# Dilated and sliding-window attention before a gated feed-forward layer: a later planned landing for transposed loads

## The chip, the core and the metric

The kernel runs on one core of a Trainium2 chip, in one launch. The metric is the time on the device in microseconds (us); the median of several runs is compared. One execution was also recorded by the hardware profiler.

## What is computed

The inputs are q, k and v (8 batches, 8 heads, 576 positions, 64 elements per head, float32), two weight matrices and a vector beta.

```python
scores = (q @ k.T) / 8                      # per batch and head
rel    = pos[:, None] - pos[None, :]
plain  = (rel >= 0) & (rel < 32)            # heads 0 to 3
dil    = (rel >= 0) & (rel < 128) & (rel % 4 == 0)   # heads 4 to 7
attn   = softmax(where(mask, scores, -1e9)) @ v
x      = attn as 4608 tokens x 512
h      = x @ w_in                           # 512 -> 2048
g      = h / (1 + exp(-beta * h))
out    = g @ w_out                          # 2048 -> 512
```

Batches are counted from 0 here, as in the code: b = 0 to 7.

## The kernel before

**Work and tiles.** Attention is done batch by batch. The feed-forward layer runs over nine tiles t of 512 tokens each; a batch has 576 tokens, so a tile takes its tokens from one or two batches. For tile t, 16 groups of four matmuls of 512 columns multiply xT (the attention's result, transposed) with w_in (`slot_h`, line 811); ScalarE takes tanh (820) and VectorE makes the gate g (825). Four blocks of 16 matmuls then multiply g with w_out (`block`, line 846), in four parts each, and the result is evacuated by ScalarE (861) or VectorE (863) and stored by an SP queue transfer (866).

**Attention of one batch.** The four dilated heads take their scores from dk and dq (line 639, matmuls on half of the array), with a tail of 16 positions per residue from the copies dkt and qt (609); the copies are made by VectorE or GpSimd (232). The four plain heads take theirs from kT and qT (673), in two halves j = 0 and 1 of the batch. ScalarE takes exp into ptd, ptt or pt (576), a mask is multiplied in (580), the values follow (714 and 699 dilated, 729 plain), and VectorE divides by the row sums (595, 596) into xdm, xdt and xsp.

**Where k and q come from.** In batches 0 to 2 (`b < DIRECT`, DIRECT = 3) TensorE transposes them. From batch 3 on, four transfers on GpSimd's queue cast them to bfloat16 in a scratch in device memory (`cast`), and four transposing transfers on the SP queue (`crossbar`, line 438) bring them back as dk, dq, kT and qT, 288 KB each. Before a batch's casts GpSimd makes a small copy (`pace`, line 924) that waits for xT of the batch two before; it keeps the transfers from starting earlier.

**The way back.** From batch 2 on the attention's result goes to device memory in two halves (`back_dma`: xdm line 483, xdt 488, xsp 475), and a transposing SP transfer per half brings it back as xT (502).

**What sets the order.** All of this is only described to `Plan`. Each operation has an engine or a choice of two, an estimated duration, dependencies and a priority `vt`; `Plan.run` goes through time, picks the next operation for the engine that can start first, and writes out the program in that order. It also picks the engine and the bank of the accumulator. For a transfer the plan takes the landing to be

```python
at = max(dma_free[e], s + d + 900)
other = max(dma_free.values()) - at
dma_free[e] = at + o.dma + max(0.0, min(o.dma, other))
o.end = dma_free[e] + (o.lat or 1100)
```

and what depends on the transfer is not placed before that planned time. `lat` is thus a constant in nanoseconds that is added to the planned landing. On the chip nothing of it remains but the order on each engine: each engine works in its order and waits for semaphores.

**Waits to know.** Batch b uses buffer b % 2 of dk, dq, kT, qT, dkt and qt. A batch's scores stand in the order among the matmuls of lines 811 and 846 of neighbouring tiles.

Of the kernel before, what the change touches and what calls it, by code (L numbers as in the profile page):

```python
# [174 lines left out]
def kernel(  # L175
# [34 lines left out]
    DIRECT = 3  # L210
# [220 lines left out]
    def crossbar(b, z, h0, deps, vt):  # L431
        kv = b % 2
        if h0:
            dst = (dk, dq)[z][kv][:].rearrange("p r h t -> p r (h t)")
        else:
            dst = qT[kv][:] if z else kT[kv][:, :, WIN:]
        src = scratch[b, z, h0][:].rearrange("(a e) -> a e", e=C * D)
        return plan.op([("SP", 1300)], lambda e: nc.sync.dma_start_transpose(out=dst, in_=src),
                       deps, vt, dma=288 * 1024 / .2 / 1000, lat=4000)

# [465 lines left out]
    def loads(b):  # L908
        if b < DIRECT:
            base = -7.25 if b == 1 else .2  # L910
            for n, (z, h0) in enumerate(((0, 4), (1, 4), (0, 0), (1, 0))):
                ld[b]["qk", z, h0] = direct_qk(b, z, h0, war(("st", z)), base + .01 * n)
            wrote(("st", 0), ("st", 1))
            ld[b]["vd"] = direct_vd(b, war("vd16"), base + .05, war(("vt", b % 2)) + [fill4])
            wrote("vd16", ("vt", b % 2))
            ld[b]["vp"] = direct_vp(b, war(("vp", b % 2)) + [fill4], base + .06)
            wrote(("vp", b % 2))
        else:
            behind = [ld[b - 1]["x", z, h0] for z in range(2) for h0 in (0, 4)] if b > DIRECT else []

            mid = (b - 2) * S + S // 2

            def t_pace(e, b=b, mid=mid):
                nc.gpsimd.tensor_copy(out=pace[:], in_=(  # L924
                    xT[0:1, 0, mid - 1:mid + 1] if b - 2 >= BY_DMA else g_t[b % 2][0:1, 0, 0:2]))
            go = plan.op([("POOL", 150)], t_pace, behind + (
                xready(mid - 1, mid + 1) if b - 2 >= BY_DMA else gop[b - 2, 0]), b - 2.4)
            for n, (z, h0) in enumerate(((0, 4), (1, 4), (0, 0), (1, 0))):
                c = cast(b, z, h0, [go], b - 2 + .01 * n)
                key = [(((("dk", "dq") if h0 else ("kT", "qT"))[z]), b % 2, i) for i in range(2)]  # L930
                ld[b]["x", z, h0] = crossbar(b, z, h0, [c] + war(*key), b - 2 + .01 * n)
                wrote(*key)
            key = [("st", z) for z in range(2)] if b < DIRECT + 2 else [("st", b % 2)]
            ld[b]["vd"] = direct_vd(b, [go] + war(*key), b - 2 + .02, [go] + war(("vt", b % 2)))
            wrote(("st", b % 2), ("vt", b % 2))
            ld[b]["vp"] = direct_vp(b, [go] + war(("vp", b % 2)), b - 2 + .03)
            wrote(("vp", b % 2))

    steady = LATER.split()
    for t in range(NTT):  # L940
# [4 lines left out]
        b = t + 1  # L945
# [46 lines left out]
```

The softmax here doesn't subtract the row's maximum and nothing guards it: scores larger than these inputs give would overflow.

## Time and profile before

| what | value |
|---|---|
| median of 5 runs | 305.62 us (305.25 to 306.92) |
| the profiled execution's own time | 305.25 us |
| span, first to last instruction | 303.5 us |
| TensorE busy (matmul) | 293.4 us, 97% of the span |
| VectorE, ScalarE, GpSimd busy | 183.6, 170.7, 90.3 us |
| mean granted TensorE clock | 1.000 |
| transposed loads dk, dq, kT, qT | 5 of each, batches 3 to 7 |

The span lies inside the execution's time; 1.75 us are outside of it. In the views, PE is TensorE, PEld its weight loads, DVE VectorE, ACT ScalarE, POOL GpSimd, and SP the engine whose queue carries transfers. Times in a view count from the start of the span. A line such as L639 is the line of the kernel that recorded the instruction; buffer numbers are left out of names, so dq stands for both of its buffers. A bracket at the end of a line in order of time gives the idle time before it and what ended it.

### The profile page before, as it was taken

What the parts mean: (1) busy time and instruction counts of PE and PEld (TensorE: products, weight loads), DVE (VectorE), ACT (ScalarE), POOL (GpSimd) and SP (SyncE); (2) the same over time, 40 slices, a digit from 0 to 9 for tenths busy, and PEclk for the clock granted to TensorE, in tenths of its full rate; (3) what the DMA queues carried; (4) which work ended last, traced back from release to release, by engine and by line L of the source; (5) the groups of instructions that cost most, each with busy time, mean ns of one, the idle gap of its engine ahead of it and who ended that gap; (6) DMA issues with size and microseconds to landing.
All of it is one profiled execution on the core that took longest, in us unless ns stands there. A gap on an engine that the chain in (4) does not pass through costs nothing.

```text
span 303.5 us, 5999 instructions
## 1 busy us (share of the span) xinstructions
PE 293.4 (97%) x2275; PEld 149.3 (49%) x2312; DVE 183.6 (61%) x422; ACT 170.7 (56%) x315; POOL 90.3 (30%) x132
## 2 busy tenths in 40 slices
PE   8899999999999989999999999999999999999995
PEld 5565456545544444444444444444444444444454
DVE  3669874988867755876677567757664344343300
ACT  2667953877548544855665566556554444554411
POOL 8988562846063107310560092100000000000000
PEclk9999999999999999999999999999999999999999
DMA  6999999999899997999999979991332100010122
GB/s 105 170 210 202 206 185 213 199 149 175 190 181 207 161 178 129 193 152 214 160 182 181 216 144 148 182 225 56 95 93 73 39 35 35 35 37 35 53 83 73
DMA packets 117376, 42.47 MB, mean 140 GB/s; under 512 B 93748, under 2 KB 110916, under 8 KB 117348
## 3 DMA queue, kind: packets, MB, share of 16 engines
q0 software_dynamic: 66672, 19.66, 63.8%
q1 hardware_dynamic: 50532, 22.36, 36.4%
q8 instruction: 18, 0.29, 0.4%
q14 instruction: 10, 0.08, 0.1%
q10 hardware_dynamic: 144, 0.07, 0.1%
HBM read 39.32 MB, written 18.87 MB: 192 GB/s over the span
## 4 chain that ended last, share of the span: by engine, by line
PE 69%; DMA 21%; POOL 4%; issue 2%; DVE 1%; SPq 1%; ACT 0%; POOLq 0%; ACTq 0%; DVEq 0%
PE bank L846 33%; PE bank L811 31%; DMA vd<-in_v_dram 4%; DMA st<-in_q_dram 4%; DMA w_in_bf<-in_moe_w_in_dram 4%; DMA st<-in_v_dram 3%; DMA dq<-s 3%; DMA x<-xsp 1%; PE bank L673 1%; PE bank L729 1%; DMA xT<-x 1%; PE bank L639 1%; POOL st L384 1%; PE bank L714 1%; POOL vp L384 1%
## 5 line engine op out<-in xcount | busy, mean ns | idle before, releaser
L846 PE MATMUL bank<-w_out_bf,g 128*128 128x512 bf16 (+2 forms) x590 | 140.2, 367 | 1.7 <-issue 1.0
L825 DVE SCALAR_TENSOR_TENSOR g<-tnh,bank 128x512 bf16<-128x512 bf16 x144 | 97.7, 685 | 72.5 <-ACT tnh L820 71.6
L820 ACT ACTIVATE tnh<-bank,beta_half 128x512 bf16<-128x512 f32 x144 | 98.5, 689 | 74.4 <-PE bank L811 70.1
L811 PE MATMUL bank<-xT,w_in_bf 128*128 128x512 bf16 (+1 forms) x565 | 139.3, 376 | 1.1 <-issue 0.2
L811 PEld LDWEIGHTS <-w_in_bf 128*128 128x128 bf16 x584 | 54.7, 98 | 60.1 <-issue 0.2
L846 PEld LDWEIGHTS <-g 128*128 128x128 bf16 x608 | 54.6, 98 | 55.7
L861 ACT ACTIVATE osb<-bank 128x512 f32<-128x512 f32 (+1 forms) x36 | 21.2, 589 | 32.0 <-PE bank L846 31.7
L576 ACT ACTIVATE pt<-bank 128x288 bf16<-128x288 f32 x64 | 21.6, 422 | 5.3 <-PE bank L673 5.3
L576 ACT ACTIVATE ptd<-bank 128x512 bf16<-128x512 f32 x32 | 17.0, 608 | 6.6 <-PE bank L639 6.6
L596 DVE TENSOR_TENSOR xsp<-bank,rcp 96x384 bf16<-96x384 f32 x32 | 17.7, 553 | 1.1
L384 POOL DMA_DIRECT2D vp<-in_v_dram x10 | 18.0, 1798 | 0.5 <-PE bank L455 0.5
L595 DVE RECIPROCAL rcp<-bank 128x4 f32<-128x4 f32 (+2 forms) x72 | 12.9, 179 | 5.3 <-PE bank L729 4.3
L580 DVE TENSOR_TENSOR ptd<-ptd,mask_d 128x512 bf16<-128x512 bf16 x27 | 12.0, 453 | 5.7 <-ACT ptd L576 4.5
L596 DVE TENSOR_TENSOR xdm<-bank,rcp 128x256 bf16<-128x256 f32 x32 | 13.6, 425 | 1.1
L384 POOL DMA_DIRECT2D vt<-in_v_dram x16 | 13.7, 1046 | 0.0
L384 POOL DMA_DIRECT2D s<-in_q_dram x10 | 13.7, 1369 | 0.0
L924 POOL COPY pace<-xT 1x2 bf16<-1x2 bf16 x4 | 0.7, 176 | 43.4 <-DMA xT<-x 36.4
L729 PEld LDWEIGHTS <-pt 128*128 128x128 bf16 x192 | 9.4, 97 | 5.9
L384 POOL DMA_DIRECT2D s<-in_k_dram x10 | 11.2, 1121 | 1.2 <-issue 1.2
L232 POOL COPY dkt<-dk 128x384 bf16<-128x384 bf16 x7 | 3.8, 548 | 25.3 <-DMA dk<-s 20.2
L729 PE MATMUL bank<-vp,pt 128*128 128x65 bf16 x192 | 10.4, 193 | 0.0
L714 PEld LDWEIGHTS <-ptd 128*128 128x128 bf16 x128 | 6.7, 98 | 4.7 <-issue 0.2
(108 smaller groups left out, 180.4 us busy)
## 6 DMA issues: line engine op xcount, KB each, us to landing
out_dram<-osb SPq DMA_DIRECT2D x35, 256.0 KB, 2.7
s<-in_k_dram POOLq DMA_DIRECT2D x10, 288.0 KB, 6.0
s<-in_q_dram POOLq DMA_DIRECT2D x10, 288.0 KB, 9.0
vp<-in_v_dram POOLq DMA_DIRECT2D x7, 384.0 KB, 17.6
w_out_bf<-in_moe_w_out_dram POOLq DMA_DIRECT2D x2, 1024.0 KB, 16.3
st<-in_k_dram POOLq DMA_DIRECT2D x6, 288.0 KB, 12.9
st<-in_q_dram POOLq DMA_DIRECT2D x6, 288.0 KB, 12.3
x<-xsp SPq DMA_DIRECT2D x12, 144.0 KB, 6.8
```

Of the source, the lines that this page charges most:

```text
L384: {"POOL": nc.gpsimd, "SP": nc.sync}[queue].dma_start(out=out, in_=in_)
L576: nc.scalar.activation(out=w(), in_=sc(), func=ACT.Exp, scale=SCALE)
L580: E[e].tensor_tensor(out=w(), in0=w(), in1=m(), op=ALU.mult)
L595: nc.vector.reciprocal(out=r, in_=p[..., D])
L596: nc.vector.tensor_tensor(out=dst, in0=p[..., 0:D], in1=r.unsqueeze(len(p.shape) - 1).to_broadcast(list(p.shape[:-1]) + [D]), op=ALU.mult)
L714: nc.tensor.matmul(pv[:, r, a], lhsT=ptd[:, x - 2, j, 2 * r + a], rhs=vd[kv][:, 2 * (x - 2) + a, 2 * r + j, 0:D + 1], start=True, stop=True)
L729: nc.tensor.matmul(pv[:, a, h2, :], lhsT=pt[x][:, (3 * j + a) * 2 + h2], rhs=vp[kv][:, (2 * x + h2) * NI + 3 * j + a, 0:D + 1], start=True ...
L811: nc.tensor.matmul(bank(g)[:, a:z], lhsT=w_in_bf[:, kt, fb * P:(fb + 1) * P], rhs=xT[:, kt, xo + a:xo + z], start=(i == 0 and kt == kts[0] ...
L820: nc.scalar.activation(out=th[:, 0:n], in_=bank(g)[:, 0:n], func=ACT.Tanh, scale=beta_half[:, fb:fb + 1])
L825: nc.vector.scalar_tensor_tensor(out=g_t[t % 2][:, fb, c0:c0 + n], in0=th[:, 0:n], scalar=1.0, in1=bank(g)[:, 0:n], op0=ALU.add, op1=ALU.mult)
L846: nc.tensor.matmul(bank(g)[:, lo:hi], lhsT=g_t[t % 2][:, fb, tb * P:(tb + 1) * P], rhs=w_out_bf[:, fb, lo:hi], start=(fb == 0), stop=(fb = ...
L861: nc.scalar.mul(out=ob[:, lo:hi], in_=bank(g)[:, lo:hi], mul=0.5)
```

## The change

The planned landing of the transposed loads of k and q gets 1500 ns later for batches 4 to 7. Batch 3 keeps the old value. No instruction is written differently; the planner places operations by the new times.

```diff
         src = scratch[b, z, h0][:].rearrange("(a e) -> a e", e=C * D)
         return plan.op([("SP", 1300)], lambda e: nc.sync.dma_start_transpose(out=dst, in_=src),
-                       deps, vt, dma=288 * 1024 / .2 / 1000, lat=4000)
+                       deps, vt, dma=288 * 1024 / .2 / 1000, lat=4000 if b == DIRECT else 5500)
```

## The prediction

> **What bounds the kernel now.** I read the page's summary first, then TensorE's waits after 60 us, then the chain of waits around the one that is left, then TensorE and the SP queue in order of time.
>
> ```profile
> span 303.5 us, 5999 instructions
> PE 293.4 (97%) x2275; PEld 149.3 (49%) x2312; DVE 183.6 (61%) x422; ACT 170.7 (56%) x315; POOL 90.3 (30%) x132
> PEclk9999999999999999999999999999999999999999
> ```
>
> TensorE is busy 97% of the span at the full granted clock, so no other engine sets the end. Its waits from 60 to 300 us (who waited for what: us in total, times, longest):
>
> ```profile
> PE bank L639 <- DMA dq<-s: 1.0, 1, 1.0
> PE bank L846 <- issue: 1.0, 6, 0.2
> ```
>
> Only the first line is a wait for data. The second is six breaks of 0.16 us where full-width matmuls follow the half-array scores. The chain places the wait (start, length, what):
>
> ```profile
> 101.12 8.31 DMA dq<-s
> 109.43 0.14 issue
> 109.57 0.62 PE bank L639 x16
> ```
>
> This is batch 4: its transposed load of dq, issued at 101.12, landed at 109.43, and the dilated scores (L639) started 0.14 later. TensorE in order of time:
>
> ```profile
> 109.57 0.62 PE L639 MATMUL bank<-dq,dk 64*128 64x128 bf16 x16 [1.04 <-DMA dq<-s]
> 139.58 0.62 PE L639 MATMUL bank<-dq,dk 64*128 64x128 bf16 x16
> 150.59 0.43 PE L673 MATMUL bank<-qT,kT 64*128 64x96 bf16 x12
> 170.39 0.62 PE L639 MATMUL bank<-dq,dk 64*128 64x128 bf16 x16
> 201.19 0.62 PE L639 MATMUL bank<-dq,dk 64*128 64x128 bf16 x16
> ```
>
> Batch 4 waits 1.04; the same scores of batches 5, 6 and 7 wait for nothing. By the trace's landing marks their dq was there at 135.28, 163.40 and 194.05: 4.3, 7.0 and 7.1 us early. So at most about 1.04 us can be gained, in one place.
>
> **What really moves.** The diff adds 1.5 us to a planned landing; only the planned order shows what follows. With the two built programs side by side, I count the big matmuls (L811 and L846) ahead of each score group. Dilated scores: batch 4 from 336 to 344, batches 5, 6, 7 unchanged at 460, 588, 716. Plain scores (L673), first and second half: batch 4 from 356 and 408 to 364 and 416; batch 5 from 504 to **480**, second half 536 unchanged; batch 6 from 632 to 636, second half unchanged; batch 7 unchanged. So the title holds for batch 4 and hardly beyond, and batch 5's first plain scores go the other way. No matmul is added or removed, and the number of half-array groups stays.
>
> **The gain.** Big matmuls start 0.216 us apart (a group of four is 0.86 in the chain). Without its wait L639 of batch 4 would start at 109.57 - 1.04 = 108.53; eight matmuls later is 108.53 + 8 x 0.216 = 110.26. dq lands at 109.43 and needs 0.14: 0.69 us to spare. The loads up to there stand in the same order on SP and POOL, so the landing has no reason to move. The wait goes whole: **-1.04**.
>
> A rule of the skill would deny that there was anything to gain. The Trainium skill, page "DMA: Bandwidth & Descriptors", section "Anatomy of one DMA — SWDGE (gpsimd) path", fits one transfer, on GpSimd's path, as 2.0 us plus bytes over 436 GB/s. As an estimate from that page, dq's 288 KB would take 2.7 us, land at 106.7 after its issue ended at 104.00, and the change would be worth 0. The row's 109.43 decides against it: the load shares the engines with casts and other transposes.
>
> **What the moves put on other queues.**
> - DVE takes batch 4's dkt copy from POOL. POOL waited for dk until 107.83; now DVE does, from about 105.66, and queued behind it are the last gate of the tile (before at 106.70) and the two qt copies. The copy is 0.54 on POOL, 0.97 in DVE's one row; the gate 0.69: done at 109.1 to 109.5. Who waits: L639, whose first bank that gate frees, at 110.26. Covered by 0.8 or more; once gone, each later us of dk costs one. Taken: 0.
> - DVE takes one output evacuation (ACT 0.60; DVE's 0.43 and 0.29 for 256 and 128 columns give an estimated 0.7 for 512). Behind it stand the four masks of batch 4's second half, the first two of which L729 needs. That half's L673 comes at 127.52 - 1.04 + 1.73 = 128.2, the block's last four matmuls end at 129.5, the evacuation at about 130.4, two masks of 0.3 at 131.0; L729 follows L673 by 3.0 as before, at 131.2. Bounds 0 to 0.3; taken 0.
> - POOL loses dkt of batch 4 (its next step, the pace copy, waits for xT until 115.3 anyway), gains batch 5's vd (1.04, from DVE) and loses half of its qt (0.29). Needed near 140, done by 133: 0.
> - SP: output stores of 0.3 to 0.6 issue go ahead of batch 4's xdm stores and of batch 6's dq and qT. dq of batch 6 has 7.0 to spare, its qT landed at 172.05 for scores at 181: 0.
> - SP, batches 5 and 7: the kT load now stands before the store of the previous batch's first half (x<-xsp), which the return transpose L502 needs.
>
> ```profile
> 127.76 0.54 SPq L475 DMA_DIRECT2D x<-xsp  x1
> 130.39 1.54 SPq L438 DMA_TRANSPOSE kT<-s  x1
> 135.88 2.09 SPq L438 DMA_TRANSPOSE qT<-s  x1
> 138.71 3.26 SPq L502 DMA_TRANSPOSE xT<-x  x1
> ```
>
> These are batch 5's loads and batch 4's store and transpose. kT landed at 139.53; the store, now behind it, lands about then, so L502 starts at about 139.6 instead of 138.71. Its own 3.26 went into a full queue (1.33 at 219.71), and it landed at 144.28; the tile's first L811 came at 145.3, now about 145.5. Bounds 0 to 0.5; taken 0. For batch 7 kT landed at 199.91, L502 stood at 197.94 for 2.69 and landed at 204.86; L811 came at 205.7 and comes now at about the same time. L502 from 199.95, for 1.33 and then the 1.9 to 4.2 that the rows have from its end to landing, gives 203.2 to 205.5; if it is late by the whole 2.0 it lands at 206.9. Bounds 0 to 1.3; taken 0, since the shorter issue pays the delay back.
> - Batch 5's plain scores, 24 matmuls forward: L673 came 11.0 us after L639, now 11.0 - 24 x 0.216 = 5.8 after it. L639 is at 139.58 - 1.04 = 138.54, so L673 at 144.3. Its qT, issued at 135.88 once the cast it reads was in, landed at 142.86: with 0.14, 1.3 to spare where there were 7.6. Bounds 0 to 3.0 (below); taken 0.
>
> **Sum.** The profiled execution took 305.25: span 303.5 and 1.75 around it. 305.25 - 1.04 = 304.21. The median of the runs is 0.37 above that execution, so 305.62 - 1.04 = 304.58. I take 0.1 more off: a later dq in the slower runs lengthens the same wait, and the new 0.69 absorbs it. **304.5**. 0.3% is 0.92 us, about what a measurement of this kernel can tell from no change: faster means under 304.70, slower over 306.54.
>
> **Rivals.**
> 1. *The wait comes back in part at batch 5's plain scores or at a tile's first L811.* For: their spare times are 1.3, about 1 and about 1 us, and they hang on loads that took 3.5 to 11.2 us from issue to landing. If qT of batch 5 takes the 8.7 us of batch 6's (163.32 to 172.05), it lands at 144.6 and costs 0.4; 0.5 more at the L811 of 145.5 brings the total back to about the old time: 304.7 to 305.6. Against: the same transfers stand ahead of qT in the queue as before, only in another order. Chance 0.28.
> 2. *Slower: batch 5's qT as late as the slowest transposed load.* kT of batch 6 took 11.24 us (158.98 to 170.22). With that, qT lands at 147.1, L673 waits 147.1 + 0.14 - 144.3 = 3.0, and the kernel ends at 305.62 - 1.04 + 3.0 = 307.6. It decides from a landing of 145.2 on (the 1.04 is spent), and over 0.3% slower from 146.1. For: before, nobody noticed how late this load came, since the scores stood 7.6 us behind it. Against: its own row says 7.0. Chance 0.20.
> 3. *The change doesn't do what it says*, so that nothing comes of it: 305.6. For: three of four batches keep their dilated scores where they were. Against: the one group that waits does move, by 1.73 us, more than its wait. Chance 0.02.
>
> The forecast, the wait gone and no new one over 0.1: chance 0.50; its own range is 303.9 to 304.7, down to 305.62 - 1.04 - 0.37 - 0.3 for runs whose dq came later than in the profile. The range takes in rival 1 and the smaller half of rival 2: 303.9 to 306.6. Faster 0.50; within 0.3% rival 1 and 3, less the little of rival 1 that may pass either edge: 0.29; slower 0.21.
>
> **What would show it.** Right: TensorE's waits have no line L639 <- DMA dq; L639 of batch 4 stands near 110.3 without idle; DVE shows a wait of about 2 us at dkt; L639 of batch 5 near 138.5; the tail of L846 ends 1.0 earlier. Wrong: a wait of L673 on qT near 144, or of L811 on xT near 145 or 206; a wait at L639 of batch 4 that remains, or one on DVE there; an L729 near 131 that waits for its masks. A slower time with none of these would overturn the whole working.

## The result, and the profile after

| kernel | median, us | lowest to highest | against before |
|---|---|---|---|
| before, 65 runs | 305.70 | 304.07 to 307.12 | |
| after, 37 runs | 304.96 | 303.98 to 306.05 | 0.9974, 95% interval 0.9965 to 0.9984 |

The change makes the kernel faster by 0.74 us between the medians, by 0.79 us (0.5 to 1.1) by the ratio. Forecast were 304.5 us: 1.04 us less for the wait and 0.1 more.

The profiled execution of after took 305.56 us, 0.31 more than that of before. That is no contradiction, as two views together show. First the summary, and TensorE's waits from 60 to 300 us, of which only this line is left:

```profile
span 303.7 us, 5999 instructions
PE 293.8 (97%) x2275; PEld 149.2 (49%) x2312; DVE 183.0 (60%) x424; ACT 171.0 (56%) x314; POOL 90.1 (30%) x131
PEclk9999999999999999999999999999999999999999
```

```profile
PE bank L846 <- issue: 0.8, 5, 0.2
```

The line L639 <- DMA dq is gone. What is left is no wait either. Each of these breaks stands before a group of L846 of which the trace has three matmuls where the program has four (or seven of eight). In b4_b6 below, whose matmuls stand in the same order, all of them are recorded and no break is seen. Behind batch 7's dilated scores, for example, after and then b4_b6:

```profile
202.16 0.81 PE L846 MATMUL bank<-w_out_bf,g 128*128 128x512 bf16 x3 [0.16 <-issue]
```

```profile
201.28 1.04 PE L846 MATMUL bank<-w_out_bf,g 128*128 128x512 bf16 x4
```

So single records are missing there, and the prediction's "six breaks of 0.16 us" were the same; no sum hung on them. TensorE in order of time, after (the dilated scores of batches 4 to 7 and batch 5's first plain ones):

```profile
111.49 0.62 PE L639 MATMUL bank<-dq,dk 64*128 64x128 bf16 x16
139.76 0.62 PE L639 MATMUL bank<-dq,dk 64*128 64x128 bf16 x16
145.59 0.43 PE L673 MATMUL bank<-qT,kT 64*128 64x96 bf16 x12
170.57 0.62 PE L639 MATMUL bank<-dq,dk 64*128 64x128 bf16 x16
201.38 0.62 PE L639 MATMUL bank<-dq,dk 64*128 64x128 bf16 x16
```

No group has a bracket, so none waited as the profile counts it. Batch 5's plain scores stand at 145.59, forward as the plan says, and do not wait either. Yet all of it is later than the prediction's 110.3 and 138.5. The reason stands long before the change: the first plain scores of batch 2 in the two kernels, before and then after.

```profile
68.22 0.43 PE L673 MATMUL bank<-qT,kT 64*128 64x96 bf16 x12
```

```profile
69.36 0.43 PE L673 MATMUL bank<-qT,kT 64*128 64x96 bf16 x12
```

Up to there both kernels have the same order, and after's execution was 1.14 late already: the waits before 60 us for input loads differ (L455 for st<-in_q was 1.1 after and 0.4 before). From this group to TensorE's last matmul it took 232.13 us before (to 300.35) and 231.17 after (to 300.53): 0.96 less. This distance is the measure used below. (Expectations that speak of 231.3 us count from the start of the L846 matmul ahead of that group, 0.31 earlier.)

The chain of waits of after, about batch 4's scores:

```profile
111.01 0.38 PE bank L846
111.39 0.10 issue
111.49 0.62 PE bank L639 x16
```

A DMA stands no longer in it. Still the load came close: by the trace's landing marks dq landed at 111.35, and L639 starts 0.14 later; from start to start TensorE lost 0.16 us more there than at the other changes from L846 to L639. VectorE's waits and the SP queue are as the working had them:

```profile
DVE dkt L232 <- DMA dk<-s: 2.3, 1, 2.3
DVE qt L232 <- DMA dq<-s: 1.3, 1, 1.3
```

```profile
128.47 2.84 SPq L438 DMA_TRANSPOSE kT<-s  x1
131.41 0.54 SPq L475 DMA_DIRECT2D x<-xsp  x1
135.10 1.99 SPq L438 DMA_TRANSPOSE qT<-s  x1
138.98 1.90 SPq L502 DMA_TRANSPOSE xT<-x  x1
```

kT now goes ahead of the store. L502 starts at 138.98, against 138.71 before, and lands at 143.12, against 144.28.

### The profile page after: what moved, and what is told of

It is laid out like the page before. It is cut to its first block, busy times and chain, and to the rows that moved or that the text cites. A ratio compares the mean times of both kernels' runs of the same rounds, so it can differ in the third digit from the quotient of the medians.

```text
span 303.7 us, 5999 instructions
## 1 busy us (share of the span) xinstructions
PE 293.8 (97%) x2275; PEld 149.2 (49%) x2312; DVE 183.0 (60%) x424; ACT 171.0 (56%) x314; POOL 90.1 (30%) x131
## 4 chain that ended last, share of the span: by engine, by line
PE 81%; DMA 11%; POOL 3%; DVE 2%; issue 2%; ACT 0%; POOLq 0%; DVEq 0%
PE bank L846 38%; PE bank L811 37%; DMA vd<-in_v_dram 4%; DMA st<-in_q_dram 4%; DMA w_in_bf<-in_moe_w_in_dram 3%; DVE g L825 2%; PE bank L729 1%; PE bank L673 1%; PE bank L639 1%; PE bank L714 1%; POOL st L384 1%; POOL vp L384 1%; PE bank L699 0%; PE bank L455 0%; DVE xdm L596 0%
## 5 line engine op out<-in xcount | busy, mean ns | idle before, releaser
L846 PE MATMUL bank<-w_out_bf,g 128*128 128x512 bf16 (+2 forms) x587 | 139.4, 367 | 1.7 <-issue 0.8
L811 PE MATMUL bank<-xT,w_in_bf 128*128 128x512 bf16 (+1 forms) x568 | 138.2, 376 | 1.2 <-DMA w_in_bf<-in_moe_w_in_dram 0.3
L811 PEld LDWEIGHTS <-w_in_bf 128*128 128x128 bf16 x584 | 55.1, 98 | 61.4 <-DMA w_in_bf<-in_moe_w_in_dram 0.4
L846 PEld LDWEIGHTS <-g 128*128 128x128 bf16 x608 | 54.4, 98 | 55.4
L729 PEld LDWEIGHTS <-pt 128*128 128x128 bf16 x192 | 9.1, 97 | 5.4
L232 POOL COPY vd<-st 128x1024 bf16<-128x1024 bf16 x5 | 5.2, 1036 | 20.5 <-DMA st<-in_v_dram 14.4
L729 PE MATMUL bank<-vp,pt 128*128 128x65 bf16 x192 | 10.1, 193 | 0.0
L863 DVE TENSOR_SCALAR osb<-bank 128x512 f32<-128x512 f32 (+2 forms) x3 | 1.4, 470 | 13.3 <-PE bank L846 13.3
```

What stands on the lines that cost most here:

```text
L232: (nc.scalar.copy if e == "ACT" else E[e].tensor_copy)(out=out, in_=in_)
L729: nc.tensor.matmul(pv[:, a, h2, :], lhsT=pt[x][:, (3 * j + a) * 2 + h2], rhs=vp[kv][:, (2 * x + h2) * NI + 3 * j + a, 0:D + 1], start=True ...
L811: nc.tensor.matmul(bank(g)[:, a:z], lhsT=w_in_bf[:, kt, fb * P:(fb + 1) * P], rhs=xT[:, kt, xo + a:xo + z], start=(i == 0 and kt == kts[0] ...
L846: nc.tensor.matmul(bank(g)[:, lo:hi], lhsT=g_t[t % 2][:, fb, tb * P:(tb + 1) * P], rhs=w_out_bf[:, fb, lo:hi], start=(fb == 0), stop=(fb = ...
```

## The experiments

Theory A: dq of batch 4 lands late against TensorE, and the gain is the wait for it, nowhere else. Theory B: the gain comes from the place of the scores or from the other batches' moves. All times are beside runs of before on the same chip. The edits are to the kernel before, to the planned `lat` of `crossbar` (line 439) unless another line is shown. The expectations name further theories, C to H.

### Batch 4 alone, and the others alone

```diff
-  lat=4000)
+  lat=5500 if b == 4 else 4000)      # only_b4
+  lat=5500 if b > 4 else 4000)       # from_b5
```

only_b4: 

> The later landing for batch 4 alone (5500 ns there, 4000 for all others). In the built order batch 4's dilated scores have 344 big matmuls ahead of them, as in the changed kernel. Theory A (the gain is the wait of batch 4's scores on dq, which eight more matmuls cover): the same time as the changed kernel, 0.7 to 1.0 us under the kernel before, and no wait of L639 over 0.3 us. Rival B (the gain needs batches 5 to 7 too): near the kernel before.

from_b5: 

> The later landing for batches 5 to 7 alone. TensorE's order stays that of the kernel before, word for word; only a few copies change between VectorE and GpSimd. Theory A: the time of the kernel before, within 0.2 us, and the wait of batch 4's L639 on dq is there again (0.5 to 2 us in the profile). Rival B: faster by 0.3 us or more.

Measured: from_b5 306.00 us against 305.59, ratio 1.0018 (0.9993 to 1.0043): no gain, as theory A has it, though the median lies 0.41 above where 0.2 was the most expected; the interval takes that in. Its trace still has the wait, 0.53 us.

```profile
109.72 0.62 PE L639 MATMUL bank<-dq,dk 64*128 64x128 bf16 x16 [0.53 <-DMA dq<-s]
```

only_b4 took 305.35 us, ratio 0.9996 (0.9968 to 1.0025). Its trace has no wait and takes 231.01 us from batch 2's scores to the end, 0.16 less than after's. But the median shows only 0.24 of it, and the interval holds both nothing and the whole gain. The runs alone leave open whether batch 4 is enough; b4_b6 below was made for that.

### The other direction, and further

```diff
-  lat=4000)
+  lat=2500 if b == 4 else 4000)          # b4_earlier
+  lat=4000 if b == DIRECT else 7000)     # later_no_forward
```

b4_earlier: 

> The opposite step: batch 4's loads planned 1500 ns earlier than in the kernel before (2500 ns). Its dilated scores have 332 big matmuls ahead of them, four fewer than before. Theory A: the wait grows by 4 x 0.216 = 0.86 us, so slower than the kernel before by 0.6 to 0.9 us, with a wait of L639 on dq of 1.5 to 2.8 us. Rival B (the position of batch 4 does not matter): the time of the kernel before.

later_no_forward: 

> 7000 ns for batches 4 to 7. Batch 4's dilated scores have 348 big matmuls ahead (twelve more than before, four more than the changed kernel); batch 5's first plain scores are no longer moved forward (508 ahead, before 504, changed kernel 480), and the store of the previous batch stands ahead of kT on the SP queue again in batches 5 and 7. Theory A: no wait at L639 of batch 4 at all, and 0 to 0.2 us faster than the changed kernel, that is 0.8 to 1.1 us under the kernel before. Rival C (the forward move of batch 5's plain scores and the new SP order carry part of the gain or of the loss): differs from the changed kernel by more than 0.3 us, with a wait in the trace after 130 us in one of the two.

later_no_forward: 304.77 us, ratio 0.9969 (0.9949 to 0.9990), no wait. With batch 5's plain scores at 508 instead of 480 the gain is the change's, so no cost of their forward move is to be seen. Rival C's sign, a wait after 130 us in one of the two kernels, does show once, in the second trace of the change (0.35 us, told under "Why the prediction was right"); but it is at L729, behind a mask, not at these scores.

b4_earlier: 308.35 us in ten runs, ratio 1.0084 (1.0047 to 1.0121). The sign is as expected, the size is not: 2.6 us by the ratio where 0.6 to 0.9 were expected. TensorE and VectorE in order of time show why a late dq costs more than its own wait here:

```profile
109.44 0.21 PE L639 MATMUL bank<-dq,dk 64*128 64x128 bf16 x1 [0.87 <-DMA dq<-s]
110.16 0.60 PE L639 MATMUL bank<-dq,dk 64*128 64x128 bf16 x15 [0.51 <-DVE g L825]
```

```profile
109.33 0.19 DVE L232 COPY qt<-dq 64x128 bf16<-64x128 bf16 x1 [2.76 <-DMA dq<-s]
109.44 0.67 DVE L825 SCALAR_TENSOR_TENSOR g<-tnh,bank 128x512 bf16<-128x512 bf16 x1
```

VectorE stands at the qt copy until dq is there, and behind it in its order is the gate g whose bank the second score needs. TensorE waits twice. The trace has 232.84 us from batch 2's scores to the end, 0.7 to 1.2 more than the three traces of the old order. The profiled execution (306.85) was among this kernel's quickest; where the others lost up to 3.8 us more, no trace shows, and most of this kernel's loss stays open.

### Batches 4 and 6, and batch 4 far back

```diff
-  lat=4000)
+  lat=5500 if b in (4,6) else 4000)      # b4_b6
+  lat=8500 if b == 4 else 4000)          # b4_far
```

b4_b6: 

> lat=5500 for batches 4 and 6, 4000 for the others. TensorE's order is that of the changed kernel matmul for matmul; against only_b4 the plain scores of batch 6 go from 608 to 636. Theory A: 0.6 to 1.1 us faster than before, no wait of L639 on dq over 0.3 us. Theory B (the forward move of batch 6's plain scores in only_b4 cost what batch 4 had gained there, 0.5 us): this one reaches 0.8, only_b4's trace would then have to show a wait at about 176 us, which it does not. Theory C (only_b4's small gain was scatter of the start-up): the trace from the L673 of batch 2 to the last matmul is within 0.2 us of only_b4's 231.3.

b4_far: 

> lat=8500 for batch 4 alone: its dilated scores stand 356 big matmuls in, 20 further than before (4.3 us), its plain ones at 396 and 420. Theory A: once the wait is gone more distance buys nothing, so 0.6 to 1.1 us faster than before like the change, spare at L639 of 2.5 us or more. Rival D (in part of its executions the change leaves a rest of the wait, as the 0.16 us in the trace after): up to 0.2 us more gain than the change. Rival E (scores that come late make the work behind them late): a new wait behind batch 4's softmax, and less gain than the change.

b4_b6: 304.97 us against 305.48, ratio 0.9980 (0.9963 to 0.9996). b4_far: 304.97 us, ratio 0.9972 (0.9957 to 0.9988). Neither trace has a wait, and from batch 2's scores to the end they take 231.05 and 231.01 us, like only_b4. So of the readings of only_b4's small gain theory C is left, the scatter of the start-up: the traced executions differ ahead of batch 2's scores and agree behind them. Its other eleven runs have no trace, so for them it is argued. Twelve more matmuls of distance (b4_far against the change) bought nothing that can be told apart, and of rival E (late scores hold up the work behind them) no wait is to be seen.

### How large the wait is

same_again is the kernel before without an edit; b4_half moves batch 4's dilated scores by half.

```diff
-  lat=4000)
+  lat=4750 if b == 4 else 4000)          # b4_half
```

same_again: 

> The before kernel once more, unchanged, for a third trace of the same order of TensorE's work. Theory A: the wait of L639 of batch 4 on dq lies between 0.3 and 1.5 us (1.0 in before, 0.5 in from_b5), set by when x<-xsp of batch 3 lands, since dk is issued 2 us behind that landing, dq 4 us behind dk, and dq lands 8.3 us after its issue. Rival F (it is the flight of dq that varies): the flight from issue to landing differs by over 0.5 us from 8.3.

change_again: 

> The changed kernel, unchanged, beside the others and for a second trace of it. Theory A (the gain is the wait of L639 of batch 4, which was 0.6, 0.7 and 1.1 us in three traces of the old order, mean 0.80, less what is left of it): 0.6 to 1.0 us faster than before; from the L673 of batch 2 to TensorE's last matmul 231.3 us plus what is left of the wait, 0 to 0.3 us.

b4_half: 

> lat=4750 for batch 4 alone: its dilated scores stand 340 big matmuls in, 4 further than before (0.86 us) instead of 8. Theory A: the waits seen in the old order (0.6, 0.7, 1.1 us) become 0, 0 and 0.24 us, so 0.5 to 0.8 us faster than before, and the trace has at most 0.3 us of it left. Rival (the wait returns with the scores, since dq lands a fixed time ahead of them): no gain.

same_again took 305.9 us, with this line:

```profile
110.16 0.62 PE L639 MATMUL bank<-dq,dk 64*128 64x128 bf16 x16 [0.62 <-DMA dq<-s]
```

The old order of TensorE's work has thus shown 1.04, 0.62 and 0.53 us, mean 0.73. (From start to start TensorE lost 1.11, 0.69 and 0.60; these are the 1.1, 0.7 and 0.6 of the expectations.) The trace on which the prediction was built had the longest of the three. dq flew 8.31, 8.62 and 8.31 us in them: theory A's 8.3 within 0.3, and rival F's 0.5 is not reached. (In the eight other traces with SP's old order it flew 8.22 to 8.90.)

b4_half took 305.27 us against 305.91, ratio 0.9983 (0.9960 to 1.0005); no wait, 231.02 us. A move of 0.86 us was enough in this execution. change_again took 305.02 us, ratio 0.9971 (0.9953 to 0.9989), and 231.37 us from batch 2's scores: dq landed 0.97 us ahead of L639, but there is another wait, of which below.

### The same gain without moving the scores back

dq is late because dk and dq stand behind L502 on SP, and L502 waits for the store x<-xsp. The views of the SP queue say so, before:

```profile
SPq L502 <- DMA x<-xsp: 3.8, 1, 3.8
```

```profile
95.10 1.80 SPq L502 DMA_TRANSPOSE xT<-x  x1
97.08 3.99 SPq L438 DMA_TRANSPOSE dk<-s  x1
101.12 2.88 SPq L438 DMA_TRANSPOSE dq<-s  x1
```

dq_first plans that store's landing later, so that the two loads go first (line 478, in `back_dma`); dq_first_later also moves batch 4's scores back:

```diff
-  [vdone[0, j], vdone[1, j]], vt_of[f"X1{j}"], dma=1200, lat=2000)]
+  [vdone[0, j], vdone[1, j]], vt_of[f"X1{j}"], dma=1200, lat=5000 if (b, j) == (3, 0) else 2000)]
...
-  deps, vt, dma=288 * 1024 / .2 / 1000, lat=4000)
+  deps, vt, dma=288 * 1024 / .2 / 1000, lat=7000 if b == 4 else 4000)     # dq_first_later only
```

dq_first: 

> The before kernel with one landing estimate changed: the x<-xsp store of batch 3's first half is planned to land 3 us later (5000 instead of 2000 ns), so that SP issues dk and dq of batch 4 ahead of the transposed load L502 of that half. The dilated scores of batch 4 are not moved back: they stand 332 big matmuls in (336 before, 344 in the changed kernel). Theory A (the wait for dq's landing is what the change takes away, and dq is late because SP's queue is held by L502, which waits for x<-xsp): dq lands before 107 us, no L639 wait on dq, and the time is 0.6 to 1.1 us below before, as in the changed kernel, with no score moved back. Theory B (it is the place of the scores in TensorE's order that makes the gain): scores at 332 as in b4_earlier, so slower than before by 1 to 3 us.

dq_first_again: 

> dq_first once more. Its trace had no wait left (231.33 us from batch 2's L673 to the last matmul, as with the change), but its median was only 0.1 us under before. Theory G (in part of its executions the transposed load qT of batch 4, which landed 113.73 there and 0.8 us ahead of the plain scores at 114.69, comes late): 0 to 0.4 us faster, and a second trace may show L673 waiting for qT. Theory C (scatter of the start-up in 12 executions): 0.6 to 1.1 us faster.

dq_first_later: 

> dq_first, and lat=7000 for batch 4: dk and dq stand ahead of L502, the dilated scores at 340 and the first plain scores at 368 (dq_first: 332 and 356), so that qT has 2.6 us more. Theory G: this gets back what dq_first lacked, 0.6 to 1.1 us faster than before, with qT landed 3 us or more ahead of L673. Theory C: the same as dq_first_again within 0.3 us. If issuing dk and dq early is bad in itself (rival H: it holds SP, and so the transposed load xT of batch 3 behind them), both stay at 0 to 0.4.

The SP queue and batch 4's scores in dq_first:

```profile
91.81 3.47 SPq L438 DMA_TRANSPOSE dk<-s  x1
95.37 3.93 SPq L438 DMA_TRANSPOSE dq<-s  x1
99.39 3.14 SPq L502 DMA_TRANSPOSE xT<-x  x1
```

```profile
108.00 0.62 PE L639 MATMUL bank<-dq,dk 64*128 64x128 bf16 x16
```

dq landed at 105.75, and the scores, 332 matmuls in as in b4_earlier, wait for nothing. Time: 305.40 against 305.48, ratio 0.9989 (0.9969 to 1.0010); once more 304.98 against 305.91, ratio 0.9969 (0.9947 to 0.9990). dq_first_later: 305.17, ratio 0.9976 (0.9956 to 0.9997). From batch 2's scores to the end the three traces take 231.02, 231.01 and 231.01 us. The first median alone was a miss and gave rise to theory G; the second fits scatter instead, and no trace has L673 waiting for qT. Rival H (early loads hold up SP) has no support either: neither trace has a wait. Against b4_earlier, with the same place and a dq that lands 3 to 4 us later, theory B falls.

### All traces side by side

Counted from the start of batch 2's L673, which is itself given in the first column. The landing marks of x<-xsp (batch 3, first half) and dq (batch 4) are the trace's; the wait is the profile's for L639 on dq.

| kernel | L639 of batch 4 at | batch 2's L673 | x<-xsp landed | dq landed | wait | to the last matmul |
|---|---|---|---|---|---|---|
| before | 336 | 68.22 | 26.83 | 41.21 | 1.04 | 232.13 |
| same_again | 336 | 69.22 | 26.12 | 40.80 | 0.62 | 231.84 |
| from_b5 | 336 | 68.88 | 26.32 | 40.71 | 0.53 | 231.62 |
| b4_earlier | 332 | 69.13 | 25.54 | 40.18 | 0.87 and 0.51 | 232.84 |
| after | 344 | 69.36 | 27.33 | 41.99 | 0 | 231.17 |
| change_again | 344 | 68.63 | 26.63 | 41.00 | 0 | 231.37 |
| only_b4 | 344 | 69.54 | 26.80 | 41.39 | 0 | 231.01 |
| b4_b6 | 344 | 68.84 | 26.70 | 41.23 | 0 | 231.05 |
| b4_half | 340 | 69.76 | 26.47 | 40.80 | 0 | 231.02 |
| later_no_forward | 348 | 68.76 | 26.83 | 41.74 | 0 | 230.96 |
| b4_far | 356 | 69.38 | 25.98 | 40.78 | 0 | 231.01 |
| dq_first | 332 | 68.62 | 25.50 | 37.13 | 0 | 231.02 |

Eight traces without any wait, with the scores anywhere from 332 to 356, agree at 231.0 us within 0.05 (dq_first_again and dq_first_later included, at 231.01 both). After is above them by the 0.16 us that it lost at L639, change_again by its other wait. The old order has 231.0 plus its wait, to some 0.2. In the eleven traces above dq_first, the landing of dq varies by 1.8 us between executions (40.18 to 41.99), and x<-xsp by as much (25.54 to 27.33); from the one to the other it is 14.3 to 14.9 us. So it is mostly the store's landing that sets how long TensorE waits, through SP's order. None of the versions without the wait can be told from the change by its runs; the best ratio, 0.9969, lies inside the change's interval.

## Why the prediction was right, and by how much it was off

**The place and the cause: right.** One wait, at L639 of batch 4, for dq; moved by more than it was long, it goes. from_b5 keeps it and gains nothing, and dq_first takes it away by the other end, with the same 231.0 us. The size fell short: 304.96 lies above the 303.9 to 304.7 of the main case, and the gain of 0.26% in the stretch that was left to rivals 1 and 3, though neither came about. So it is the room made for the rivals that let the range hold, and that is luck in part.

**The term of -1.04: too large.** It was one execution's wait taken for all. Three traces of the old order have 1.04, 0.62 and 0.53. Their mean 0.73, less the 0 to 0.16 that was left of it in the two traces of the change, is 0.6 to 0.7; measured were 0.74 to 0.79 with 0.5 to 1.1 around it.

**"The landing has no reason to move": wrong.** Nothing moved it in the order, but it moves from execution to execution. The old order has no wait if dq lands by about 40.1 (109.57 - 1.11 - 0.14 - 68.22, with 1.11 the loss from start to start). None of the eleven traces with SP's old order of dk and dq behind L502 is under that. The new place has 1.73 more, up to 41.8: after itself, at 41.99, is the one trace beyond it, by its 0.16. The 0.69 to spare was about the spread.

**The 0.1 for a later dq in slower runs: not borne out.** It took the profiled wait for a short one; the other two traces have shorter ones.

**VectorE's side: mostly right.** The wait of dkt is 2.3 and 1.7 us in the change's two traces ("about 2"), the evacuation took 0.69 ("an estimated 0.7"), the gate behind dkt was done ahead of L639. The dkt copy itself took 0.36 on VectorE, not the 0.97 of its one row before. The masks behind the evacuation were taken at 0.3 each with bounds 0 to 0.3 for L729. That step lacked a partner: in the POOL point the working gave batch 5's vd copy, moved from VectorE to GpSimd, the price 0, "needed near 140". In change_again it ran beside the first of those masks, and pushed the dkt copy behind it onto the second. VectorE, GpSimd and TensorE in order of time:

```profile
130.59 1.68 DVE L580 TENSOR_TENSOR pt<-pt,maskn_PP 128x288 bf16<-128x288 bf16 x4
```

```profile
130.06 1.04 POOL L232 COPY vd<-st 128x1024 bf16<-128x1024 bf16 x1 [6.64 <-DMA st<-in_v_dram]
131.04 0.62 POOL L232 COPY dkt<-dk 128x384 bf16<-128x384 bf16 x1
```

```profile
131.88 0.33 PE L729 MATMUL bank<-vp,pt 128*128 128x65 bf16 x5 [0.18 <-DVE pt L580]
```

The first two masks took 0.67 and 0.64 us, and L729 lost 0.35 from start to start, which is the 231.37 of that trace. In after's trace the vd copy had been done at 129.52, and the same masks took 0.30 or 0.31 each:

```profile
131.48 0.96 DVE L580 TENSOR_TENSOR pt<-pt,maskn_PP 128x288 bf16<-128x288 bf16 x4
```

In b4_b6 the first mask was held as long (0.68), the second was not (0.30), and L729 did not wait. So a price that was put at 0 is 0 in one trace and 0.35 in another.

**SP's side: right.** L502 of batch 4 was due at 139.6 and came at 138.98; that of batch 6 was due at 199.95, came at 200.63 and landed at 204.97, inside the 203.2 to 205.5. Neither of the two L811 waits. The bound had a row missing, though: from L502's end to landing the profile before has up to 6.43 (96.90 to 103.33), not 4.2.

**Batch 5's plain scores: right, with more to spare than feared.** qT landed at 141.71, 3.9 us ahead of 145.59, where 1.3 were worked out: it was issued at 135.10, ahead of 135.88, in spite of the later start, and took 6.6 us to land. Rivals 1 and 2 hung on it, and neither came about; rival 3 falls with from_b5 and only_b4's traces. The slowest transposed load before was dq of batch 5 (11.36), not kT of batch 6 (11.24), which moves the bound of rival 2 by 0.1.

## What to carry to other kernels

A wait that one profiled execution shows is a draw: before it is counted as a gain, look in a second and third trace how long it is, and follow the late transfer back along its queue to what varies (here a store two places ahead). Compare traces from a point that both kernels reach with the same order, since the start-up alone differed by 1.5 us here, twice the gain. Where only a late landing is at fault, putting its issue ahead of a waiting one in the queue did the same here as moving the consumer back; and behind a waiting copy on another engine, look for the bank that the waiting matmuls need next.

## What was not expected of the hardware

**A mask is held by GpSimd's copy.** In change_again the masks begun at 130.59 and 131.18 ended at 131.26 and 131.82, 0.16 and 0.17 us after a GpSimd copy had ended (131.10 and 131.66); a mask alone takes 0.30. In the fourteen traces, after 60 us, 26 masks began while GpSimd copied vd or dkt: 23 ended 0.16 or 0.17 us after the copy, the longest taking 1.17, two began with under 0.1 of the copy left, and one, begun within 0.01 of the copy's start, kept its 0.31. Masks that had begun by themselves and were running when the copy began kept 0.30 or 0.31, and where 0.2 us or more of one was left it was the copy that took longer (only_b4's dkt of 131.54 took 0.66, after's 0.54). The evacuation L863 of only_b4, begun at 130.89 within GpSimd's copy of 130.22 to 131.26, kept its 0.69. The Trainium skill, page "SBUF — State Buffer", section "Terms", calls the port pair of VectorE and GpSimd an exclusive lock whose loser blocks altogether, and page "GPSIMD Engine Reference", section "1. Specifications", names VectorE's instructions with two SBUF inputs; the masks read two, the evacuation reads an accumulator bank, and these rows agree with both, but for the one mask that kept its 0.31.

**A small store was slow among another engine's transfers.** Before's x<-xsp of 144 KB was issued at 87.23, between GpSimd's casts and loads of batch 4 (85.97 to 91.41), and landed at 95.05: 7.8 us; the other half's, issued at 107.65, took 3.1. The Trainium skill, page "DMA: Bandwidth & Descriptors", section "Issuing engines are not separate DMA queues", has transfers of all issuing engines run on the same 16 DMA engines and interleave; the two rows agree, but no run here took the loads away, so the cause is not shown.
